# Attention without GpSimd's tensor work, the single query tile last, another cycle of steps, the first chunk's expert matmuls in the attention's plan

## The chip, the cores and the metric

The kernel runs on one core of a Trainium2 chip. The metric is the device time of one execution in microseconds (us), the median of several runs. A core has five engines, each of which takes its instructions in order: TensorE (PE in the profile; PEld is its weight load), VectorE (DVE), ScalarE (ACT), GpSimd (POOL) and SyncE (SP), which here only starts transfers. Engines wait for each other through semaphores. SBUF is the on-chip memory that all of them read and write; PSUM holds TensorE's results.

## The reference

```python
scores = scale * np.matmul(q, k.transpose(0, 1, 3, 2))       # (4, 8, 576, 576), head_dim 64
thresh = np.max(scores, axis=-1, keepdims=True) - tau
scores = np.where(scores >= thresh, scores, -1000000000.0)
scores = scores - np.max(scores, axis=-1, keepdims=True)
attn = np.exp(scores)
attn = attn / (np.sum(attn, axis=-1, keepdims=True) + 1e-09)
x = np.matmul(attn, v)                                        # then (2304, 512)
...
h = x @ w_in                                                  # expert 1: 512 -> 2048 -> 512
x = (np.maximum(h, 0.0) + alpha * np.minimum(h, 0.0)) @ w_out
h = x @ w_in2                                                 # expert 2
out = (h * (1.0 / (1.0 + np.exp(-h)))) @ w_out2
```

The weights of both experts arrive as 64-bit floats and are brought to 32 bits on the chip. Every 32-bit product of the experts is made of three matmuls of a rounded part and a rest (`TERMS`).

## The kernel before

**Attention.** The 32 heads are worked in 16 pairs. The 576 queries of a pair are nine tiles, t = 0 to 8: tiles 0 to 7 hold 128 queries of one head each, two by two (even t for the one head, odd t for the other), and tile 8, the single one, holds the last 64 queries of both. For each tile TensorE makes the scores (`qkmm`, L333) in PSUM; VectorE copies them to SBUF scaled and takes the row maximum in the same instruction (`maxi`, L347); ScalarE takes the exponential (`expo`, L360) and a threshold from maximum and tau (`thr`, L367); VectorE masks by the threshold and sums the row (`mask`, L373). TensorE then transposes the masked tile into PSUM (`trans`, L408) and ScalarE copies it to SBUF (`copy`, L123). The sums' reciprocals (`recip`, L382) are spread over 64 columns by a broadcast copy (`spread`, L388, on GpSimd) and are transposed too (`transr`, L414). TensorE multiplies with the values (`pv`, L442, in five steps; `pv8`, L449, for the single tile), and VectorE multiplies by the transposed reciprocals into `X` (`evac`, L456; `evac8`, L463).

**The order.** All of this stands in a manual schedule. `CYCLE` lists TensorE's steps for one turn, each with an offset in pairs: Q is a score step, T a bank of transposes, Tr and Rr the leftover columns and the spread reciprocals, P a value step. `line` repeats it over the pairs, and TensorE issues in exactly this order. `plan()` walks the engines in time, with a duration and a priority for every operation, and so sets the order of the other four. Before the change a pair's tiles come in the order 8, 0, 1, ... 7. Score tiles share two PSUM buffers (`psS`), so a score step waits for the row maxima of the tiles two places earlier.

**Other work in the plan.** Four of the eight weight tiles that the first expert needs first are converted during the attention (`conv`, `wconv`, WN = 4, from score step 60 on, every 12 steps). One conversion is a 0.5 MB transfer and nine operations: ScalarE L157, VectorE L159, L161, L163, ScalarE L165, L167, GpSimd L169 and L171, VectorE L173. The first token chunk of 512 is split into its two parts there too (`xh`, `xl`, L545 and L548).

**Experts.** The second part is left to the tile framework's scheduler, which orders all engines by its own estimates and may place its instructions among the attention's. A job is one of 2 experts, 4 groups of hidden units and 5 chunks of tokens (four of 512, one of 256). In a job each of the four hidden blocks takes 12 matmuls (`mm_h`, L202) into a PSUM tile of `psH` (4 buffers), an activation (`act1`: ScalarE L211, VectorE L212; `act2`: L221, L222), a split (L123, L119), and, three blocks later (`LAG`), the output matmuls (`ymm`, L590 or L599). Chunks are split by ScalarE and GpSimd (`xsplit`), and the remaining weights are converted here with the same `wconv`.

Of the kernel before, what the change touches and what calls it, by code (L numbers as in the profile page):

```python
# [8 lines left out]
F32 = mybir.dt.float32  # L9
# [14 lines left out]
G = 4  # L24
# [16 lines left out]
WT = 30  # L41
# [54 lines left out]
def attn_moe_moe(  # L96
# [52 lines left out]
    def wconv(stage, pool, wi, wo, g, j):  # L149
# [82 lines left out]
    wA, xs0 = [], {}  # L232

    with ExitStack() as pa:
# [9 lines left out]
        psS = ent(name="psS", bufs=2, space=PSUM)  # L244
# [24 lines left out]
        seq = [(i, t) for i in range(NP) for t in (8, 0, 1, 2, 3, 4, 5, 6, 7)]  # L269
# [114 lines left out]
        def spread(i, ch):  # L384
# [6 lines left out]
        line = [(x, i + o) for i in range(-1, NP + 1) for x, o in cycle if 0 <= i + o < NP]  # L391
# [80 lines left out]
        def conv(j, after):  # L472
            it = wconv(stage, (wpa, wpo)[j // NC], w1i, w1o, 0, j)
# [13 lines left out]
        op(("tauv",), "DVE", 0.3, -1, [("ld", 0, 1)], setv)  # L487
# [186 lines left out]
```

## Time and profile before

| | us |
|---|---|
| median of 3 runs (1094.64 to 1097.5) | 1095.68 |
| the profiled execution's own time | 1095.02 |
| span of its instructions in the profile | 1093.2 |
| TensorE busy | 1077.0 (99%) |
| VectorE, ScalarE, GpSimd busy | 745.0, 599.1, 413.6 |

The attention takes the first 307 us of the span and the experts the rest. "Busy" is the union of an engine's instructions; matmuls are pipelined and overlap in the record, so the pace of TensorE is read from start to start and not from the length of one. In a timeline a bracket behind a row names the time that the engine stood idle ahead of it, and what ended that.

### The profile page before, as it was taken

Reading aid. Unit: us, or ns where it says so; the run is one execution under the profiler, and the core shown is the slowest. Engines: PE = TensorE matmul, PEld = TensorE weight load, DVE = VectorE, ACT = ScalarE, POOL = GpSimd, SP = SyncE. Lnnn points to the kernel's source line nnn. Section 1 sums busy time; section 2 is a strip of 40 time slices with the busy share of each in tenths; the row PEclk is TensorE's granted clock in tenths of the full one; section 3 lists DMA queues with packets and bytes.
Section 4 is the critical chain, followed back from the end, with each engine's and each line's share of the span. In section 5 each row is a group of like instructions: output and inputs, shape, how many; then the busy total and the mean of one; then the engine's idle time right before and its main releaser. Section 6 shows DMA issues by size and latency. Waiting matters only on the chain.

```text
span 1093.2 us, 15460 instructions
## 1 busy us (share of the span) xinstructions
PE 1077.0 (99%) x5705; PEld 837.9 (77%) x5705; DVE 745.0 (68%) x1382; ACT 599.1 (55%) x1129; POOL 413.6 (38%) x339
## 2 busy tenths in 40 slices
PE   8999999999999999999999999999999999999998
PEld 5666656556767888888888888888888888888887
DVE  6989999989456677848755883764378568634343
ACT  5777878877555765535533553564555445334321
POOL 0100131320155566528525662662365346424210
PEclk8999999999999999999999999999999999999999
DMA  3212222211022222201110120121012002000112
GB/s 105 65 60 65 79 84 85 79 60 41 19 78 77 77 62 75 77 1 58 63 34 20 60 77 1 39 78 39 1 58 78 20 20 78 1 1 1 39 58 77
DMA packets 19259, 57.10 MB, mean 52 GB/s; under 512 B 2416, under 2 KB 2544, under 8 KB 19184
## 3 DMA queue, kind: packets, MB, share of 16 engines
q1 hardware_dynamic: 18880, 55.84, 15.8%
q8 instruction: 45, 0.74, 0.3%
q10 hardware_dynamic: 304, 0.28, 0.1%
q14 instruction: 30, 0.25, 0.1%
HBM read 51.39 MB, written 4.72 MB: 51 GB/s over the span
## 4 chain that ended last, share of the span: by engine, by line
PE 74%; DVE 6%; issue 3%; POOL 2%; ACT 2%; DMA 0%; DVEq 0%; POOLq 0%; ACTq 0%; SPq 0%
PE h L202 33%; PE y L599 18%; PE y L590 14%; PE s L333 3%; PE pv L442 3%; PE t L408 3%; DVE e L373 2%; POOL we L171 1%; DVE x L347 1%; DVE wa L161 1%; POOL wa L169 1%; DVE w L173 0%; ACT acc L228 0%; DVE wm L159 0%; DVE r L212 0%
## 5 line engine op out<-in xcount | busy, mean ns | idle before, releaser
L202 PE MATMUL h<-xs,w 128*128 128x512 f32 (+1 forms) x1920 | 431.1, 368 | 3.1 <-DVE r L212 3.1
L202 PEld LDWEIGHTS h<-xs,w 128*128 128x128 f32 x1920 | 337.8, 188 | 66.2 <-DVE r L212 4.9
L590 PE MATMUL y<-g,w 128*128 128x512 f32 (+1 forms) x960 | 215.0, 368 | 0.4 <-ACT acc L228 0.4
L599 PE MATMUL y<-w,g 128*128 128x512 f32 x864 | 213.7, 390 | 0.0
L590 PEld LDWEIGHTS y<-g,w 128*128 128x128 f32 x960 | 169.0, 188 | 31.6 <-ACT acc L228 0.7
L599 PEld LDWEIGHTS y<-w,g 128*128 128x128 f32 x864 | 160.7, 188 | 32.4
L119 DVE TENSOR_TENSOR g<-r,g 128x512 fp32r<-128x512 f32 (+1 forms) x160 | 140.7, 879 | 52.4 <-ACT g L123 51.1
L169 POOL TENSOR_TENSOR wa<-wa,w 128x512 f32<-128x512 f32 x64 | 84.0, 1313 | 207.3 <-ACT w L165 86.2
L119 POOL TENSOR_TENSOR xs<-acc,xs 128x512 fp32r<-128x512 f32 (+1 forms) x80 | 106.5, 1361 | 133.2 <-ACT xs L123 133.1
L123 ACT ACTIVATE g<-r 128x512 fp32r<-128x512 f32 (+1 forms) x160 | 94.0, 588 | 90.0 <-DVE r L222 46.6
L119 POOL TENSOR_TENSOR xs<-X,xs 128x512 fp32r<-128x512 f32 (+1 forms) x76 | 104.2, 1399 | 57.5 <-ACT xs L123 57.3
L347 DVE TENSOR_SCALAR_CACHE_REDUCE x<-s,nsc 128x576 f32<-128x576 f32 x144 | 112.4, 815 | 13.0 <-PE s L333 11.5
L360 ACT ACTIVATE e<-x,m 128x576 f32<-128x576 f32 x128 | 96.3, 781 | 43.5 <-DVE x L347 42.9
L373 DVE SCALAR_TENSOR_TENSOR e<-x,m,e 128x577 f32<-128x577 f32 x128 | 110.1, 881 | 8.1 <-ACT m L367 7.7
L222 DVE TENSOR_TENSOR r<-h,r 128x512 f32<-128x512 f32 (+1 forms) x80 | 50.7, 634 | 95.0 <-ACT r L221 94.9
L333 PE MATMUL s<-raw 64*128 64x288 f32 (+1 forms) x576 | 110.3, 437 | 5.1 <-DVE x L347 4.3
L388 POOL COPY rb<-m 128x256 f32<-128x256 f32 (+1 forms) x48 | 27.6, 576 | 211.8 <-PE t L414 100.3
L173 DVE TENSOR_TENSOR w<-we,wa 128x512 fp32r<-128x512 f32 x64 | 58.7, 918 | 61.1 <-POOL we L171 52.0
L221 ACT ACTIVATE r<-h 128x512 f32<-128x512 f32 (+1 forms) x80 | 43.8, 548 | 102.5 <-PE h L202 102.0
L171 POOL TENSOR_TENSOR we<-we,wm 128x512 f32<-128x512 f32 x64 | 93.6, 1462 | 13.7 <-ACT wm L167 13.1
L212 DVE SCALAR_TENSOR_TENSOR r<-r,neg,h 128x512 f32<-128x512 f32 (+1 forms) x80 | 55.0, 689 | 48.6 <-ACT r L211 48.4
L165 ACT ACTIVATE w<-wa 128x512 fp32r<-128x512 f32 x64 | 40.5, 633 | 82.2 <-DVE wa L161 75.4
(63 smaller groups left out, 1054.9 us busy)
## 6 DMA issues: line engine op xcount, KB each, us to landing
wraw<-in_w1i SPq DMA_DIRECT2D x16, 512.0 KB, 3.7
wraw<-in_w1o SPq DMA_DIRECT2D x16, 512.0 KB, 3.4
wraw<-in_w2i SPq DMA_DIRECT2D x16, 512.0 KB, 3.6
wraw<-in_w2o SPq DMA_DIRECT2D x16, 512.0 KB, 3.5
rv<-in_v SPq DMA_DIRECT2D x16, 480.0 KB, 3.4
raw<-in_q SPq DMA_DIRECT2D x15, 320.0 KB, 3.2
out<-o SPq DMA_DIRECT2D x18, 256.0 KB, 2.0
raw<-in_k SPq DMA_DIRECT2D x15, 288.0 KB, 2.8
```

Of the source, the lines that this page charges most:

```text
L119: le.tensor_tensor(out=lo, in0=src, in1=hi.bitcast(F32), op=ALU.subtract)
L123: e.activation(out=dst, in_=src, func=AF.Copy)
L169: nc.gpsimd.tensor_tensor(out=a, in0=a, in1=w[:, 0].bitcast(F32), op=ALU.subtract)
L171: nc.gpsimd.tensor_tensor(out=e, in0=e, in1=m, op=ALU.mult)
L173: V.tensor_tensor(out=w[:, 1], in0=e, in1=a, op=ALU.add)
L202: nc.tensor.matmul(ps[:, :n], w[c][:, a, fl * 128:(fl + 1) * 128], xs[c][:, b, :n], start=k == 0, stop=k == 3 * NC - 1,)
L333: T.matmul(SP[u + k][:, hf, :S // 2], RAW[i][p, 0, q], RAW[i][p, 1, c], start=True, stop=True)
L347: V.tensor_scalar(out=x.rearrange("p (a b) -> p a b", a=2), in0=SP[u][:, :, :S // 2], scalar1=nsc, scalar2=None, op0=ALU.mult, op1=ALU.min ...
L360: A.activation(out=ES[u], in_=xts[u % XB][:, 1:S + 1], func=AF.Exp, bias=mcol(u, 0), scale=-1.0)
L373: V.scalar_tensor_tensor(out=e, in0=x, scalar=mcol(u, 1), in1=e, op0=ALU.is_le, op1=ALU.mult, accum_out=mcol(u, 2))
L590: nc.tensor.matmul(ys[e][:, :n], w[NC + fl][:, a, e * 128:(e + 1) * 128], gt[:, c, :n], start=fl == 0 and k == 0, stop=fl == G - 1 and k == 2,
L599: nc.tensor.matmul(ys[s], gt[:, a, s * 128:(s + 1) * 128], w[NC + fl][:, c, :], start=fl == 0 and k == 0, stop=fl == G - 1 and k == 2,)
```

## The change

- The single tile comes last in a pair (order 0, 1, ... 8), and `CYCLE` is another list of the same steps. The first loads are ordered for it: the first 128 query columns come first, and tau's transfer is third instead of second on ScalarE's queue; pair 1's loads wait for the first score step.
- The broadcast of the reciprocals goes from GpSimd to ScalarE, as an activation.
- In the planned conversions GpSimd's two operations go to VectorE (the expert stage keeps them on GpSimd). The first four conversions start at score step 20, every 14 steps; the other four, of the output weights, are planned as well and start 4 score steps before the last.
- The first two chunks' splits are planned (ScalarE and VectorE).
- The first chunk's 48 hidden matmuls are operations of the plan (name "h"), which may fill TensorE's waits from the last row maxima on; their PSUM tiles come from `psS`, now two buffers of two blocks, which also takes the place of `psH` in all jobs.
- The expert stage's pools reuse memory with waits by tile (`reuse_waits="tile"`). A few planned durations and priorities differ.

```diff
-WI = 60
+WI = 20
+WT = 4
-WS = 12
+WS = 14
...
-    "P8:0 Q6:0 P1:-1 P2:-1 Rr1:-1 T1:0 Q8:1 T2:0 T3:0 "
+    "P0:-2 P1:-2 P2:-2 Q6:-1 T3:-1 T4:-1 T1:-1 Q8:-1 Tr8:-2 "
...
+        if e == "PE":
+            c = [n for n in c if n == seq[pe]] or [n for n in c if n[0] == "h"]
+            fill = [n for n in cand[e] if n[0] == "h"]
+            if fill and c != fill and ready[c[0]] > max(free[e], ready[fill[0]]) + ops[fill[0]][1]:
+                c = fill
...
-        nc.gpsimd.tensor_tensor(out=a, in0=a, in1=w[:, 0].bitcast(F32), op=ALU.subtract)
-        yield
-        nc.gpsimd.tensor_tensor(out=e, in0=e, in1=m, op=ALU.mult)
+        e2.tensor_tensor(out=a, in0=a, in1=w[:, 0].bitcast(F32), op=ALU.subtract)
+        yield
+        e2.tensor_tensor(out=e, in0=e, in1=m, op=ALU.mult)
...
-        seq = [(i, t) for i in range(NP) for t in (8, 0, 1, 2, 3, 4, 5, 6, 7)]
+        seq = [(i, t) for i in range(NP) for t in range(9)]
...
+            nc.sync.dma_start(raw(0)[:, 0, :128], src[0][:, :128])
+            nc.sync.dma_start(raw(0)[h0, 0, 128:], src[0][h0, 128:])
+            A.dma_start(raw(0)[h1, 0, 128:], src[0][h1, 128:])
             A.dma_start(sc[:, 0:1], tau[0:1].unsqueeze(0).to_broadcast([128, 1]))
...
-            P.tensor_copy(RS[i, ch][:, :n], stat(i)[:, 2, a:z].unsqueeze(2).to_broadcast([128, n, 64]))
+            A.activation(out=RS[i, ch][:, :n], in_=stat(i)[:, 2, a:z].unsqueeze(2).to_broadcast([128, n, 64]), func=AF.Copy)
...
-        for j in range(WN):
-            conv(j, [qk(WI + j * WS if j < NC else NU - WT)])
+        for j in range(NC + G):
+            conv(j, [qk(WI + j * WS if j < WN else NU - WT)])
...
+                need = [("h", f, c - 1)] if c else [("h", f - 1, NC - 1), ("max", NU - 2 + f // 2)]
+                op(("h", f, c), "PE", 0.68, 0, need + [("xl", 0, c), ("w", c, 9)], go, 0.9)
...
-        psH = ent(name="psH", bufs=4, space=PSUM)
...
-                ps = psH.tile([128, 512], F32, tag="h", name="h")
-                mm_h(ps, w, fl, xs, n)
+                if fl % 2 == 0:
+                    hp = hs0[fl] if (m, g, t0) == (1, 0, 0) else psS.tile([128, 2, 512], F32, tag="s", name="s")
+                ps = hp[:, fl % 2]
+                if (m, g, t0) != (1, 0, 0):
+                    mm_h(ps, w, fl, xs, n)
```

What stands on TensorE in the middle of the attention, for most of one cycle; `s` are scores, `t` transposes, `pv`, `p` and `q` value steps. Before:

```order
L333 MATMUL s<-raw 128x288 x4
L442 MATMUL pv<-pt,rv 64x512 x4
L414 MATMUL t<-ident,rb 128x128 x2
L408 MATMUL t<-ident,e 128x128 x4
L333 MATMUL s<-raw 128x288 x2
L408 MATMUL t<-ident,e 128x128 x12
L333 MATMUL s<-raw 128x288 x4
L442 MATMUL pv<-pt,rv 64x512 x2
L442 MATMUL pv<-px,rv 64x512 x2
L408 MATMUL t<-ident,e 128x128 x8
L333 MATMUL s<-raw 128x288 x4
L408 MATMUL t<-ident,z 128x128 x4
```

And after, on the same engine and in the same stage:

```order
L448 MATMUL pv<-pt,rv 64x512 x6
L339 MATMUL s<-raw 128x288 x4
L414 MATMUL t<-ident,e 128x128 x12
L339 MATMUL s<-raw 128x288 x2
L414 MATMUL t<-ident,z 128x128
L414 MATMUL t<-ident,e 128x128 x6
L420 MATMUL t<-ident,rb 128x128 x3
L339 MATMUL s<-raw 128x288 x4
L448 MATMUL pv<-pt,rv 64x512 x2
L455 MATMUL t<-p_1237,rv 64x64 x8
L455 MATMUL t<-q_1312,rv 64x64 x2
L448 MATMUL pv<-px,rv 64x512 x2
```

A whole cycle before has four runs of two-tile score steps, four of transposes (the single tile's scores, two matmuls, stand inside one of them) and three of value steps; after it has four, three and two.

The end of the attention on TensorE; `h` and, after, `s<-xs,w` are the first expert's hidden matmuls, `y` its output matmuls. Before:

```order
L408 MATMUL t<-ident,e 128x128 x4
L202 MATMUL h<-xs,w 128x512 x11
L408 MATMUL t<-ident,e 128x128 x2
L414 MATMUL t<-ident,rb 128x128 x2
L408 MATMUL t<-ident,e 128x128 x2
L202 MATMUL h<-xs,w 128x512 x5
L442 MATMUL pv<-pt,rv 64x512 x6
L414 MATMUL t<-ident,rb 128x128 x2
L442 MATMUL pv<-pt,rv 64x512 x2
L442 MATMUL pv<-px,rv 64x512 x2
L202 MATMUL h<-xs,w 128x512 x42
L590 MATMUL y<-g,w 128x512 x8
```

After:

```order
L448 MATMUL pv<-pt,rv 64x512 x6
L414 MATMUL t<-ident,z 128x128
L420 MATMUL t<-ident,rb 128x128
L448 MATMUL pv<-pt,rv 64x512 x2
L455 MATMUL t<-p_2973,rv 64x64 x8
L455 MATMUL t<-q_2994,rv 64x64 x2
L448 MATMUL pv<-px,rv 64x512 x2
L208 MATMUL s<-xs,w 128x512 x48
L616 MATMUL y<-g,w 128x512 x12
L208 MATMUL s<-xs,w 128x512 x12
L616 MATMUL y<-g,w 128x512 x24
L208 MATMUL s<-xs,w 128x512 x12
```

Before, 48 hidden matmuls stand among the last transposes and 42 follow the attention; after, no hidden matmul stands among the attention's steps, and 48 follow its last value step in one run.

A conversion in the middle of the attention. Before, on GpSimd, between the spread copies (`rb`):

```order
L388 COPY rb<-m 128x128
L388 COPY rb<-m 128x256
L169 TENSOR_TENSOR wa<-wa,w 128x512
L388 COPY rb<-m 128x256
L171 TENSOR_TENSOR we<-we,wm 128x512
L388 COPY rb<-m 128x128
```

After, on VectorE, where row maxima are L353, masks L379 and reciprocals L388:

```order
L379 SCALAR_TENSOR_TENSOR e,m<-x_119,m,e 128x577
L175 TENSOR_TENSOR wa<-wa,w 128x512
L353 TENSOR_SCALAR x_128,m<-s,nsc 128x576
L353 TENSOR_SCALAR x_119,m<-s,nsc 128x576
L379 SCALAR_TENSOR_TENSOR e,m<-x_122,m,e 128x577
L379 SCALAR_TENSOR_TENSOR e,m<-x_125,m,e 128x577
L379 SCALAR_TENSOR_TENSOR e,m<-x_128,m,e 128x577
L388 RECIPROCAL m<-m 128x4
L379 SCALAR_TENSOR_TENSOR e,m<-x_119,m,e 128x577
L353 TENSOR_SCALAR x_122,m<-s,nsc 128x576
L353 TENSOR_SCALAR x_125,m<-s,nsc 128x576
L177 TENSOR_TENSOR we<-we,wm 128x512
```

The two operations now stand between masks and maxima in VectorE's own queue, and GpSimd has nothing between its first instructions and the expert stage.

## Rows read from the trace of the kernel before

**Rows 1.** The page's busy time by engine (busy us, share of the span, instructions).

```profile
PE 1077.0 (99%) x5705; PEld 837.9 (77%) x5705; DVE 745.0 (68%) x1382; ACT 599.1 (55%) x1129; POOL 413.6 (38%) x339
```

**Rows 2.** Busy time of each engine in stretches of the attention: the stretch and its length in us, then busy us and (x instructions) of PE, PEld, DVE, ACT and POOL, the granted clock as a share of full speed, the DMA share and GB/s. The second and third are one cycle each, from one spread copy to the same copy of the next pair; the first covers six cycles, the last is the sixth of them.

```profile
121.46:233.47 112.01, 106.80 (x734) 63.79 (x732) 106.26 (x272) 89.87 (x176) 29.20 (x31) 0.98 0.23 75
87.42:104.44 17.02, 17.02 (x124) 10.57 (x123) 15.22 (x43) 13.30 (x27) 1.65 (x3) 1.00 0.20 63
121.46:138.48 17.02, 17.02 (x125) 10.55 (x123) 16.42 (x46) 14.41 (x29) 3.48 (x4) 1.00 0.21 68
210.38:233.47 23.09, 19.73 (x118) 10.46 (x117) 20.28 (x47) 16.27 (x33) 9.57 (x9) 0.93 0.12 36
```

**Rows 3.** The timeline of TensorE in one undisturbed cycle: start us, busy us, engine, line, tiles, count. The record counts each 32-bit score, value and small value matmul as two.

```profile
90.07 1.57 PE L333 MATMUL s<-raw 64*128 64x288 f32 x8
91.57 1.08 PE L442 MATMUL pv<-pt,rv 128*64 128x512 f32 x4
...
93.44 1.09 PE L408 MATMUL t<-ident,e 128*128 128x128 f32 x8
94.46 1.24 PE L333 MATMUL s<-raw 64*128 64x288 f32 x8
95.63 0.66 PE L408 MATMUL t<-ident,z 128*128 128x128 f32 x4
...
99.01 0.44 PE L408 MATMUL t<-ident,e 128*128 128x128 f32 x2
99.38 1.08 PE L442 MATMUL pv<-pt,rv 128*64 128x512 f32 x4
100.29 0.63 PE L449 MATMUL t<-p,rv 128*64 128x64 f32 x16
```

**Rows 4.** VectorE's maxima and masks between 20 and 260 us by line (count, then duration in ns, smallest, median and largest, and the first and last start), and four rows of the timeline of GpSimd and VectorE at one conversion.

```profile
L347 DVE TENSOR_SCALAR_CACHE_REDUCE x<-s,nsc x124: 782/816/821, 19.6 to 259.6; 128x576 f32<-128x576 f32 x124
L373 DVE SCALAR_TENSOR_TENSOR e<-x,m,e x108: 786/817/1824, 21.2 to 257.9; 128x577 f32<-128x577 f32 x108
```

```profile
138.48 0.83 POOL L388 COPY rb<-m 128x256 f32<-128x256 f32 x1 [0.70 <-PE t L414]
138.99 0.94 DVE L373 SCALAR_TENSOR_TENSOR e<-x,m,e 128x577 f32<-128x577 f32 x1
139.28 1.78 POOL L171 TENSOR_TENSOR we<-we,wm 128x512 f32<-128x512 f32 x1
139.86 1.82 DVE L373 SCALAR_TENSOR_TENSOR e<-x,m,e 128x577 f32<-128x577 f32 x1
```

**Rows 5.** VectorE's groups of the conversions between 20 and 260 us (line, engine, operation, tiles, shapes, count, busy us, mean ns of one, idle us before).

```profile
L161 DVE SCALAR_TENSOR_TENSOR wa<-wraw,wm 128x512 int32<-128x512 int32 x4 | 3.0, 738 | 0.0
L173 DVE TENSOR_TENSOR w<-we,wa 128x512 fp32r<-128x512 f32 x4 | 2.7, 680 | 0.0
L163 DVE TENSOR_SCALAR we<-wa 128x512 int32<-128x512 int32 x4 | 2.1, 520 | 0.0
L159 DVE TENSOR_SCALAR wm<-wm 128x512 int32<-128x512 int32 x4 | 1.7, 414 | 0.0
```

**Rows 6.** The timeline of GpSimd in the longest cycle.

```profile
217.40 5.88 POOL L119 TENSOR_TENSOR xs<-X,xs 128x512 fp32r<-128x512 f32 x4 [4.44 <-ACT xs L123]
```

**Rows 7.** The start: rows of the timeline (tau's transfer, its first user, the first mask, the second pair's second score step), and a stretch of TensorE alone (length, busy us and count of PE, clock, DMA share, GB/s).

```profile
1.34 0.87 ACTq L313 DMA_DIRECT2D sc<-in_tau  x1
5.63 0.15 DVE L137 TENSOR_SCALAR ge<-sc 128x1 f32<-128x1 f32 x1 [4.22 <-DMA sc<-in_tau]
7.96 0.82 DVE L373 SCALAR_TENSOR_TENSOR z<-x,m,z 128x577 f32<-128x577 f32 x1 [1.03 <-ACT m L367]
25.68 1.93 PE L333 MATMUL s<-raw 64*128 64x288 f32 x8
```

```profile
12.00:16.00 4.00, 4.00 (x16) 0.50 0.00 0
```

**Rows 8.** The end of the attention and the hand-over: rows of TensorE's timeline (the last pair's second score step; the first and the last of five groups that hold 48 hidden matmuls, of 18, 9, 5, 11 and 5; the last value step; the first rows of the experts), two stretches with the columns of rows 2, and the activation's two groups from 306 us on with the columns of rows 5.

```profile
274.58 1.24 PE L333 MATMUL s<-raw 64*128 64x288 f32 x8
...
285.19 4.38 PE L202 MATMUL h<-xs,w 128*128 128x512 f32 x18
...
300.39 1.39 PE L202 MATMUL h<-xs,w 128*128 128x512 f32 x5
...
305.71 1.03 PE L442 MATMUL pv<-px,rv 128*64 128x512 f32 x4
308.27 9.81 PE L202 MATMUL h<-xs,w 128*128 128x512 f32 x42 [1.53 <-DVE r L212]
317.92 1.98 PE L590 MATMUL y<-g,w 128*128 128x512 f32 x8
...
343.17 3.01 PE L202 MATMUL h<-xs,w 128*128 128x512 f32 x12 [1.32 <-DVE r L212]
```

```profile
306.00:345.00 39.00, 35.86 (x156) 28.39 (x153) 25.15 (x36) 22.43 (x41) 19.64 (x16) 1.00 0.26 83
345.00:1090.00 745.00, 743.67 (x3546) 625.75 (x3544) 460.60 (x639) 349.20 (x647) 342.11 (x253) 1.00 0.14 44
```

```profile
L212 DVE SCALAR_TENSOR_TENSOR r<-r,neg,h 128x512 f32<-128x512 f32 x64 | 47.3, 742 | 26.4 <-ACT r L211 26.2
L211 ACT ACTIVATE r<-h 128x512 f32<-128x512 f32 x64 | 37.5, 588 | 28.5 <-PE h L202 21.5 <-DVE g L119 5.2 <-PE pv L442 1.3
```

More of the change, by code (lines that the diff above doesn't have):

```diff
@@ L196, in xsplit, with mm_h @@
         return xs
-    def mm_h(ps, w, fl, xs, n):
-        k = 0
-        for c in range(NC):
+    def mm_h(ps, w, fl, xs, n, cs=range(NC)):
+        k = 3 * cs[0]
+        for c in cs:
             for a, b in TERMS:
@@ L230, in accum @@
             V.tensor_tensor(out=dst, in0=ps, in1=dst, op=ALU.add)
-    wA, xs0 = [], {}
+    psS = ctx.enter_context(tc.tile_pool(name="psS", bufs=2, space=PSUM))
+    wA, xs0, hs0 = [], [{}, {}], {}
     with ExitStack() as pa:
@@ L387, in spread @@
             RS[i, ch] = rbp.tile([128, 4, 64], F32, tag="rb", name="rb")
-            P.tensor_copy(RS[i, ch][:, :n], stat(i)[:, 2, a:z].unsqueeze(2).to_broadcast([128, n, 64]))
+            A.activation(out=RS[i, ch][:, :n], in_=stat(i)[:, 2, a:z].unsqueeze(2).to_broadcast([128, n, 64]), func=AF.Copy)
         cycle = [(x.split(":")[0], int(x.split(":")[1])) for x in CYCLE.split()]
-        line = [(x, i + o) for i in range(-1, NP + 1) for x, o in cycle if 0 <= i + o < NP]
+        line = [(x, i + o) for i in range(0, NP + 2) for x, o in cycle if 0 <= i + o < NP]
         banks = []
@@ L472, in conv @@
         def conv(j, after):
-            it = wconv(stage, (wpa, wpo)[j // NC], w1i, w1o, 0, j)
+            it = wconv(stage, (wpa, wpo)[j // NC], w1i, w1o, 0, j, V)
             prev = after
@@ L537, in attn_moe_moe @@
                 order["pv", i, kt] = ("pv", i, kt - 1)
-            op(("evac", i), "DVE", 0.62, 0, [("pv", i, KT - 1)], lambda i=i: evac(i), 0.78)
-        WOPS = [("SP", 0.6)] + [("ACT", 0.52), ("DVE", 0.34), ("DVE", 0.61), ("DVE", 0.34), ("ACT", 0.52), ("ACT", 0.52), ("POOL", 1.23), ("POOL", 1.23), ("DVE", 0.61)]
-        for j in range(WN):
-            conv(j, [qk(WI + j * WS if j < NC else NU - WT)])
-        for c in range(NC):
-            def hi0(c=c):
-                xs0[c] = bx.tile([128, 2, 512], F32R, tag="xs", name="xs")
-                one(A, xs0[c][:, 0], X[:, c, :512])
-            op(("xh", c), "ACT", 0.52, 9, [("evac", c), qk(NU - XO)], hi0)
-            op(("xl", c), "DVE", 0.61, 9, [("xh", c)], lambda c=c: V.tensor_tensor(out=xs0[c][:, 1], in0=X[:, c, :512], in1=xs0[c][:, 0].bitcast(F32), op=ALU.subtract))
+            op(("evac", i), "DVE", 0.62, -1, [("pv", i, KT - 1)], lambda i=i: evac(i), 0.78)
@@ new lines, in attn_moe_moe, with hi, lo @@
+        WOPS = [("SP", 0.6)] + [("ACT", 0.52), ("DVE", 0.34), ("DVE", 0.61), ("DVE", 0.34), ("ACT", 0.52), ("ACT", 0.52), ("DVE", 0.61), ("DVE", 0.61), ("DVE", 0.61)]
+        for j in range(NC + G):
+            conv(j, [qk(WI + j * WS if j < WN else NU - WT)])
+        for ch in range(2):
+            for c in range(NC):
+                t0, n = CH[ch]
+                def hi(ch=ch, c=c, t0=t0):
+                    xs0[ch][c] = bx.tile([128, 2, 512], F32R, tag="xs", name="xs")
+                    one(A, xs0[ch][c][:, 0], X[:, c, t0:t0 + 512])
+                def lo(ch=ch, c=c, t0=t0):
+                    x = xs0[ch][c]
+                    V.tensor_tensor(out=x[:, 1], in0=X[:, c, t0:t0 + 512], in1=x[:, 0].bitcast(F32), op=ALU.subtract)
+                src = [("evac", c), qk(NU - XO)] + ([("evac8", c), ("evac", HP + c), qk(NU - 1), ("xh", 0, c)] if ch else [])
+                op(("xh", ch, c), "ACT", 0.52, 9, src, hi, 0.72)
+                op(("xl", ch, c), "DVE", 0.61, 9, [("xh", ch, c)], lo, 0.8)
@@ new lines, in attn_moe_moe, with go @@
+        for f in range(G):
+            for c in range(NC):
+                def go(f=f, c=c):
+                    if f % 2 == 0 and c == 0:
+                        hs0[f] = psS.tile([128, 2, 512], F32, tag="s", name="s")
+                    mm_h(hs0[f - f % 2][:, f % 2], wA, f, [xs0[0][x] for x in range(NC)], 512, (c,))
+                need = [("h", f, c - 1)] if c else [("h", f - 1, NC - 1), ("max", NU - 2 + f // 2)]
+                op(("h", f, c), "PE", 0.68, 0, need + [("xl", 0, c), ("w", c, 9)], go, 0.9)
+                order["h", f, c] = need[0]
@@ L616, in attn_moe_moe @@
             oi = order.index((m, g))
-            if xs0:
-                xs = [xs0.pop(c) for c in range(NC)]
+            if (m, g) == (1, 0) and t0 < 1024:
+                xs = [xs0[t0 // 512][c] for c in range(NC)]
             else:
```

41 lines of the change are left out of this document (19 added, 22 removed), and 4 rows, old and new, of the table CYCLE.

## The prediction

> **What bounds the kernel now.** I read the page's busy times first, then the engines stretch by stretch, then TensorE's timeline inside one cycle of the attention, and last the two ends of the attention. TensorE is busy for 99% of the span [rows 1], so the question is what each of its microseconds is spent on. In the expert stage there is nothing to win: from 345 to 1090 us it stands idle for 1.3 us in all, at full clock [rows 8], and the change leaves it the same matmuls. In an undisturbed cycle of the attention it is busy for all of 17.02 us, while VectorE has 15.22 and ScalarE 13.30 [rows 2]. So TensorE's own stream sets the cycle. Six cycles in the middle take 112.01 us where six undisturbed ones would take 102.1: 9.9 us are lost there, and in the longest TensorE is idle for 3.4 us and its clock is at 0.93 [rows 2]. The sum below is made against the profiled execution's 1095.0 us, which is 0.7 under the median of the runs; I add 0.7 at the end.
>
> **The change part by part.**
>
> Fewer runs on TensorE. The pace is read from start to start. Eight transposes take 94.46 - 93.44 = 1.02 us and two take 99.38 - 99.01 = 0.37, so each costs 0.108 and the run itself about 0.15 [rows 3]. Eight value matmuls take 93.44 - 91.57 = 1.87 and four that are followed by more value work take 0.91 [rows 3], which leaves about the same 0.1 to 0.2 for a run of these. The new cycle has one run of transposes and one of value steps less and the same matmuls: -0.30 per cycle. Between the second score step of the second pair and that of the last lie 14 cycles: **-4.2**, from -2.8 to -5.6 with 0.1 to 0.2 for a run. One wait is left in the cycle: the score step behind the single tile takes 91.57 - 90.07 = 1.50 us where another takes 95.63 - 94.46 = 1.17 [rows 3]. After the change that step still stands behind the single tile and transposes (10, where there were 12), so I keep the 0.33.
>
> Conversions and chunk split off GpSimd. The 9.9 us of the six cycles go: a mask beside GpSimd's conversion took 1.82 us where the median is 0.82 [rows 4], and four chunk splits held GpSimd for 5.88 us [rows 6] with spread copies queued behind them: **-9.9**.
>
> Conversions on VectorE. A conversion now has six VectorE operations, the four of [rows 5] and two more like L173: 0.74 + 0.52 + 0.41 + 3 x 0.68 = 3.7, or 3.3 by starts, since each overlaps the next by some 0.07 to 0.08 (a maximum repeats at 0.74 and is recorded as 0.82 [rows 4]). VectorE is free for 16.7 - 15.1 = 1.6 us in a cycle of 16.7, and a conversion comes every 14 of 9 score tiles, every 1.56 cycles: 2.5 us of room for 3.3. It is short by 0.8, and I take 1.0 each, four times: **+4.0**. The lower end is 0: a cycle with VectorE at 16.42 was not a bit longer [rows 2]. The upper is all of it, 4 x 3.3 = +13.
>
> [...] The spread copies' effect is in the rows: the mask beside a copy of 0.83 us took 0.94, 0.13 more than the median [rows 4], so taking GpSimd's 1.65 us of copies per cycle away frees VectorE by about 0.1. [...]
>
> First chunk's split, four operations like L173 at 0.68 on VectorE inside two cycles with 3.2 us of room: **+0.5** (0 to 2.7). The second chunk's split comes after the last maxima, when VectorE has no more scores to take. The spread as an activation: three per cycle; even at GpSimd's 1.65 us they fit ScalarE's room of 17.02 - 13.30 = 3.7 [rows 2]: hidden, **0**, up to +2 if exponentials wait behind them.
>
> The start. Tau's transfer, which lets the first maximum go, started at 1.34 us and was waited for until 5.63 [rows 7]; third in its queue, it comes about half a microsecond later, so the first maximum starts near 6.7. By the new order VectorE has 11 maxima and 8 masks ahead of the second pair's second score step: 19 x 0.74 = 14.1, with reciprocals 14.3. The first mask of before waited 1.03 for ScalarE [rows 7]; I take four such waits: 25.0 where it was 25.68, **-0.7**. Pair 1's loads now wait for the first score step; from there they have some 17 us until that pair's own first one, and tau's transfer took 4.3 from start to landing: hidden. Without waits beyond 1.7 it is 22.7 (-3); with the clock at 0.50, as from 12 to 16 us of before [rows 7], the score steps take twice as long and it is 26.7 (+1).
>
> The end. From the last pair's second score step (274.58) to the last value step's end (305.71 + 1.03) are 32.2 us, of which 48 hidden matmuls take 48 x 0.23 = 11.0 (42 take 317.92 - 308.27 = 9.65): 21.1 for the attention [rows 8]. The new order works a pair later in the cycle. After that score step there is the rest of a cycle without the next pair's score step, 16.7 - 1.2 = 15.5, and a last turn of 26 transposes (3.1 with their runs), 12 value matmuls (2.8 at the rate of [rows 3]) and 8 with the 20 small ones (1.87 + 0.63 [rows 3]), 8.4, plus 1.0 of waits, since the order shows no hidden matmul that fills them: 24.9. **+3.8** (2.8 to 6).
>
> The hand-over. TensorE waited 1.53 and 1.32 us there, with 0.3 between [rows 8]. Now 48 hidden matmuls, 11 us, stand between the last value step and the first output matmul, and the activations run beside them; but VectorE has three conversions of the output weights in its queue, and behind them the activations. I leave 1.0 of 3.1: **-2.1** (-3 to +5).
>
> Sum: -4.2 - 9.9 + 4.0 + 0.5 + 0 - 0.7 + 3.8 - 2.1 = -8.6, which gives 1086.4 for the profiled execution and **1087** for the median.
>
> **The rivals.**
>
> All meshes. VectorE takes the conversions in its gaps (4.0 less), the 0.33 of each cycle goes (4.6 less) and the start is at its early end (2.3 less): **1076**. For it speaks the cycle with 16.42 us on VectorE that was not lengthened [rows 2]; against it that 15.1 + 3.3 / 1.56 = 17.2 us of VectorE do not go into 16.7.
>
> VectorE becomes the bound. It is at 90% now and at 103% by that last number while conversions run. Then the shorter stream of TensorE buys nothing (4.2 more) and a conversion costs 2.0 instead of 1.0 (4.0 more): **1095**, and up to 1100 with all of it on the path. That is mostly no change that a measurement of this kernel can tell, which begins at about 0.3%.
>
> Slower: the paired PSUM tiles. Before, a hidden block's PSUM tile was freed alone, four in turn; now two blocks share one, two in turn, and the first block of a new pair waits until VectorE has read the second of the pair before last. If that is on the path once in each of 39 jobs, the price is the activation, 0.59 + 0.74 = 1.3 us [rows 8], 52 us in all: **1139**. From 8.6 / 39 = 0.22 us per job it eats the gain. Against it: in the new order 12 or more output matmuls, 2.8 us, stand between a pair and its reuse.
>
> [...]
>
> **How the numbers follow.** The forecast of 1087 (1083 to 1092) has 0.60; all meshes 0.15; VectorE the bound 0.18; the paired tiles 0.05; the clock 0.02. Faster by over 0.3% means under 1092.4: 0.58 of the forecast, 0.15 and 0.03 of the third, 0.76. Slower, over 1099: 0.05 of the third and the last two, 0.12. The same: 0.12. The range leaves out the two slow cases, the top of the third and the lower half of the second: 1076 to 1096.
>
> **What would show it.** Right: undisturbed cycles of 16.6 to 16.9 us with TensorE busy throughout; cycles with a conversion of at most 17.7; masks never over 0.85 us in the attention; the second pair's second score step near 25; the attention's last value step ending near 289 without hidden matmuls before it; idle time of TensorE under 3 us from there to 345. Wrong: TensorE waiting for maxima in every cycle (VectorE the bound), hidden matmuls waiting for the activation in each job, or a clock below 1.00 after 345.

## The result and the profile after

The changed kernel takes 1104.42 us (median of four runs, 1103.04 to 1105.28) where the kernel before takes 1095.16 beside it: a ratio of 1.0083, 95% interval 1.0058 to 1.0108. It is slower by 0.8%; 1087 was forecast, with a range from 1076 to 1096.

The page's busy times of the changed kernel, against [rows 1]: TensorE has lost 2% of its share of the span, and GpSimd's tensor work starts behind the attention.

```profile
span 1103.5 us, 15284 instructions
...
PE 1072.2 (97%) x5705; PEld 835.7 (76%) x5705; DVE 750.3 (68%) x1402; ACT 606.8 (55%) x1177; POOL 353.8 (32%) x271
```

Cut where the prediction cut it: the 14 cycles from the second pair's second score step to the last pair's, the end up to the last value step, the 48 hidden matmuls, the hand-over, the expert stage. Windows of the changed kernel: length, then busy us of TensorE, its weight loads, VectorE, ScalarE, GpSimd, the granted clock, DMA share and GB/s.

```profile
25.05:255.80 230.75, 230.75 (x1708) 144.49 (x1709) 221.50 (x619) 201.77 (x426) 0.00 (x0) 1.00 0.23 73
255.80:280.18 24.38, 24.09 (x182) 14.30 (x180) 20.86 (x57) 20.69 (x43) 0.00 (x0) 1.00 0.18 64
280.18:291.20 11.02, 11.02 (x50) 9.12 (x49) 8.06 (x13) 5.62 (x10) 3.01 (x3) 1.00 0.55 180
291.20:345.00 53.80, 48.06 (x201) 38.36 (x200) 40.14 (x56) 31.47 (x57) 29.12 (x20) 0.97 0.20 63
345.00:1090.00 745.00, 728.82 (x3452) 609.72 (x3451) 439.54 (x599) 333.81 (x617) 320.73 (x243) 1.00 0.12 39
```

The attention did better than forecast and the expert stage far worse. The first row is 14 cycles of 16.48 us with TensorE busy in all of it; before they took 274.58 - 25.68 = 248.90 [rows 7, 8]. In the last row TensorE stands idle for 16.2 us, where [rows 8] has 1.3. Against the spans (1103.5 and 1093.2):

| part | before | after | difference | forecast |
|---|---|---|---|---|
| to the second pair's second score step | 25.68 | 25.05 | -0.6 | -0.7 |
| 14 cycles | 248.90 | 230.75 | -18.2 | -9.6 |
| the end, with 48 hidden matmuls | 32.16 | 35.40 | +3.2 | +3.8 |
| from there to the end of the span | 786.5 | 812.3 | +25.8 | -2.1 |

The last line begins at 306.74 before and at 291.20 after; from either on the same matmuls are left, all but 48 hidden ones. So 25.8 us were lost on the same work. TensorE's waits in the changed kernel, from 290 to 345 us and then from 345 to 1090 (total, times, longest). L208 is the hidden matmul, L616 and L625 are the output matmuls, L218 and L228 VectorE's step that reads a hidden block from PSUM in the first and second expert layer.

```profile
PE y L616 <- DVE g L125: 2.8, 2, 1.9
PE s L208 <- DVE r L218: 2.7, 1, 2.7
PE y L616 <- ACT g L129: 0.2, 1, 0.2
```

```profile
PE s L208 <- DVE r L218: 6.0, 4, 1.8
PE s L208 <- DVE r L228: 4.7, 4, 1.6
PE y L616 <- DVE acc L236: 2.7, 2, 1.3
PE y L625 <- DVE acc L236: 1.3, 1, 1.3
PE y L616 <- ACT acc L234: 1.0, 1, 1.0
PE y L625 <- DVE X L236: 0.5, 1, 0.5
```

Nine waits, 13.4 us, are hidden matmuls that wait for the reading of an earlier hidden block: the paired PSUM tiles, which the prediction gave 0.05. All waits together are 21.9 us; before, the same stretch has 3.5, of which 3.1 are in [rows 8]. One of them from the timeline of all engines (start, length, engine, line, operation, in brackets the idle time before and who ended it):

```profile
519.27 1.98 PE L208 MATMUL s<-xs,w 128*128 128x512 f32 x8
...
521.08 2.88 PE L616 MATMUL y<-g,w 128*128 128x512 f32 x12
...
522.61 0.69 ACT L163 ACTIVATE wm<-wraw 128x512 f32<-128x512 f32 x1 [2.44 <-POOL we L177]
...
523.19 1.08 ACT L217 ACTIVATE r<-s 128x512 f32<-128x512 f32 x2
...
523.79 0.69 DVE L167 SCALAR_TENSOR_TENSOR wa<-wraw,wm 128x512 int32<-128x512 int32 x1
...
524.52 0.43 DVE L169 TENSOR_SCALAR we<-wa 128x512 int32<-128x512 int32 x1
524.86 0.74 DVE L218 SCALAR_TENSOR_TENSOR r<-r,neg,s 128x512 f32<-128x512 f32 x1
...
525.66 1.19 PE L208 MATMUL s<-xs,w 128*128 128x512 f32 x4 [1.69 <-DVE r L218]
```

The block that the next pair waits for (the second of s_4961 in the listing below) ends one matmul, 0.23 us, before the output matmuls start: at 520.85. Its reading does not begin then. ScalarE is held until 522.61 by the first step of a weight conversion (L163), which waits for GpSimd, and the activation stands behind it; VectorE then has two more steps of the conversion (L167, L169) ahead of its own. Its step starts at 524.86 and ends at 525.60, 4.75 us after the block. TensorE had one hidden and 12 output matmuls to do meanwhile, until 525.66 - 1.69 = 523.97, which is 3.1 us. At 525.66 it goes on. The other eight waits look the same: in each an L163 that GpSimd had held stands just ahead of the activation on ScalarE, a conversion's step stands just ahead of VectorE's, and the reading ends 2.9 to 6.9 us after the block.

In program order on TensorE (the numbers tell the tiles apart) these blocks stand so:

```
1374 L208 MATMUL s_4961<-xs_4945,w_4000 128x512 [waits DVE_49]
...
1410 L208 MATMUL s_5022<-xs_4945,w_4000 128x512 [waits DVE_49]
...
1415 L208 MATMUL s_4961<-xs_4945,w_4000 128x512 [waits DVE_49]
...
1427 L208 MATMUL s_5103<-xs_5087,w_4000 128x512 [waits DVE_49]
```

Tile s_4961 gets its first block, then s_5022 its first but for one matmul, and only then s_4961 its second. In the code the second block of a pair comes behind the activation of the first, and its matmuls carry a wait for VectorE's reading of that first block. So two tiles stand filled at about the same time, both still to be read, when the next pair (s_5103) needs one.

### The profile page after: what moved, and what is told of

Same layout as the page of the kernel before. It is cut to its first block, busy times and chain, and to the rows that moved or that the text cites. A ratio compares the mean times of both kernels' runs of the same rounds, so it can differ in the third digit from the quotient of the medians.

```text
span 1103.5 us, 15284 instructions
## 1 busy us (share of the span) xinstructions
PE 1072.2 (97%) x5705; PEld 835.7 (76%) x5705; DVE 750.3 (68%) x1402; ACT 606.8 (55%) x1177; POOL 353.8 (32%) x271
## 4 chain that ended last, share of the span: by engine, by line
PE 73%; DVE 12%; POOL 6%; issue 5%; ACT 3%; DMA 0%; DVEq 0%; POOLq 0%; ACTq 0%; SPq 0%
PE s L208 25%; PE y L625 13%; PE y L616 11%; PE s L339 8%; PE t L414 7%; PE pv L448 6%; POOL we L177 3%; DVE g L125 2%; DVE wa L167 2%; DVE w L179 2%; POOL wa L175 2%; POOL xs L125 2%; DVE wm L165 1%; DVE r L218 1%; ACT w L171 1%
## 5 line engine op out<-in xcount | busy, mean ns | idle before, releaser
L208 PE MATMUL s<-xs,w 128*128 128x512 f32 (+1 forms) x1920 | 420.6, 371 | 13.3 <-DVE r L218 8.6
L208 PEld LDWEIGHTS s<-xs,w 128*128 128x128 f32 x1920 | 339.5, 190 | 81.0 <-DVE r L218 10.8
L175 POOL TENSOR_TENSOR wa<-wa,w 128x512 f32<-128x512 f32 x56 | 75.4, 1346 | 459.1 <-ACT w L171 346.2
L616 PE MATMUL y<-g,w 128*128 128x512 f32 (+1 forms) x960 | 210.1, 369 | 6.8 <-DVE g L125 2.8
L625 PE MATMUL y<-w,g 128*128 128x512 f32 x864 | 207.5, 390 | 1.8 <-DVE acc L236 1.3
L616 PEld LDWEIGHTS y<-g,w 128*128 128x128 f32 x960 | 167.3, 189 | 38.0 <-DVE g L125 3.7
L625 PEld LDWEIGHTS y<-w,g 128*128 128x128 f32 x864 | 160.9, 188 | 35.7 <-ACT r L227 1.5
L125 DVE TENSOR_TENSOR g<-r,g 128x512 fp32r<-128x512 f32 (+1 forms) x160 | 154.2, 978 | 27.1 <-ACT g L129 25.0
L228 DVE TENSOR_TENSOR r<-s,r 128x512 f32<-128x512 f32 (+1 forms) x80 | 49.0, 632 | 110.0 <-ACT r L227 109.8
L353 DVE TENSOR_SCALAR_CACHE_REDUCE x<-s,nsc 128x576 f32<-128x576 f32 x144 | 112.5, 816 | 12.9 <-PE s L339 11.9
L218 DVE SCALAR_TENSOR_TENSOR r<-r,neg,s 128x512 f32<-128x512 f32 (+1 forms) x80 | 53.8, 688 | 71.5 <-ACT r L217 71.3
L379 DVE SCALAR_TENSOR_TENSOR e<-x,m,e 128x577 f32<-128x577 f32 x128 | 99.7, 812 | 1.0 <-ACT m L373 1.0
L171 ACT ACTIVATE w<-wa 128x512 fp32r<-128x512 f32 x64 | 40.6, 635 | 97.2 <-DVE wa L167 74.4
L339 PEld LDWEIGHTS s<-raw 64*128 64x128 f32 (+1 forms) x576 | 59.6, 192 | 44.6 <-DVE e L379 12.2
L163 ACT ACTIVATE wm<-wraw 128x512 f32<-128x512 f32 x64 | 43.3, 677 | 87.5 <-POOL we L177 80.8
L227 ACT ACTIVATE r<-s 128x512 f32<-128x512 f32 (+1 forms) x80 | 41.3, 548 | 88.1 <-PE s L208 87.7
```

Of the source, the lines that this page charges most:

```text
L125: le.tensor_tensor(out=lo, in0=src, in1=hi.bitcast(F32), op=ALU.subtract)
L175: e2.tensor_tensor(out=a, in0=a, in1=w[:, 0].bitcast(F32), op=ALU.subtract)
L208: nc.tensor.matmul(ps[:, :n], w[c][:, a, fl * 128:(fl + 1) * 128], xs[c][:, b, :n], start=k == 0, stop=k == 3 * NC - 1,)
L339: T.matmul(SP[u + k][:, hf, :S // 2], RAW[i][p, 0, q], RAW[i][p, 1, c], start=True, stop=True)
L353: V.tensor_scalar(out=x.rearrange("p (a b) -> p a b", a=2), in0=SP[u][:, :, :S // 2], scalar1=nsc, scalar2=None, op0=ALU.mult, op1=ALU.min ...
L379: V.scalar_tensor_tensor(out=e, in0=x, scalar=mcol(u, 1), in1=e, op0=ALU.is_le, op1=ALU.mult, accum_out=mcol(u, 2))
```

## The experiments

Times are medians of four runs; ratios are to the kernel before, run beside them. It took 1095.09 beside the tile for each block, the pairs in the kernel before, the run without tile-wise waits and the output weights after the attention; 1095.28 beside the output weights along the attention, the two runs back on GpSimd and the kernel before with nothing of this on GpSimd; 1095.36 beside the other four. These differ by under 0.03%, so medians are compared across them.

**A tile for each hidden block.** The attention's tiles of two blocks are given up after the first job, and four tiles of one block take their place.

```diff
...
-                if fl % 2 == 0:
-                    hp = hs0[fl] if (m, g, t0) == (1, 0, 0) else psS.tile([128, 2, 512], F32, tag="s", name="s")
-                ps = hp[:, fl % 2]
...
+                    if psH is None:
+                        sS.close()
+                        psH = ent(name="psH", bufs=4, space=PSUM, side="right")
+                    ps = psH.tile([128, 512], F32, tag="h", name="h")
...
```

> The changed kernel, in which hidden blocks after the first job have a PSUM tile each again, four in turn; all else as changed. Theory (paired tiles): the hidden blocks' nine waits for the activation's two steps on VectorE, 13.3 us by the list of waits, go, and part of the output matmuls' waits behind them: 1084 to 1090. Rival (the conversions' steps on ScalarE and VectorE stand in front of the activations whatever the tiles): the waits move to other instructions and 1100 or more stays. Attention's last value step near 280 in both.

Measured: 1083.08, ratio 0.9892 (0.9875 to 0.9909), 21.3 us less than the changed kernel. TensorE's only waits from 290 to 1090 us, and its expert stage by the windows:

```profile
PE y L617 <- DVE g L125: 5.2, 2, 4.6
```

```profile
291.30:345.00 53.70, 48.49 (x203) 39.26 (x202) 43.17 (x58) 33.79 (x63) 31.28 (x22) 0.94 0.21 69
345.00:1070.00 725.00, 725.00 (x3461) 610.91 (x3460) 435.35 (x601) 332.01 (x613) 325.04 (x241) 1.00 0.12 39
```

From 345 us on TensorE is never idle. The activations are still late in that stage (one block's two steps start at 520.37 on ScalarE and only at 524.40 on VectorE), so the conversions in front of them cost nothing by themselves. The rest of this kernel's loss is at the hand-over.

**Pairs in the kernel before.** One edit the other way round:

```diff
-        psH = ent(name="psH", bufs=4, space=PSUM)
+        psH = ent(name="psH", bufs=2, space=PSUM)
...
-                ps = psH.tile([128, 512], F32, tag="h", name="h")
+                if fl % 2 == 0:
+                    hp = psH.tile([128, 2, 512], F32, tag="h", name="h")
+                ps = hp[:, fl % 2]
```

> The kernel before with one edit: hidden blocks in pairs, two PSUM tiles of two banks in turn. Theory (paired tiles): 13 to 20 us slower than the kernel before, 1107 to 1115, with waits of 1 to 2 us of hidden matmuls for VectorE's activation step in most of the jobs. Rival (the loss comes from how attention's new end joins the expert stage): within 3 us of the kernel before.

Measured: 1120.18, ratio 1.0226 (1.0203 to 1.0248): 25.1 us slower, more than the 13 to 20 expected. The first waits from 345 to 1090 us are nearly those of the changed kernel:

```profile
PE h L202 <- DVE r L212: 6.7, 5, 1.8
PE h L202 <- DVE r L222: 4.6, 4, 1.6
PE y L590 <- DVE acc L230: 2.7, 2, 1.4
```

The pairs alone cost it, without anything else of the change.

**Pairs with both blocks together.** The pair stays; only the order in the program is another, both blocks' matmuls and then both activations.

```diff
                 if fl % 2 == 0:
                     hp = hs0[fl] if (m, g, t0) == (1, 0, 0) else psS.tile([128, 2, 512], F32, tag="s", name="s")
+                    for x in range(2):
+                        if (m, g, t0) != (1, 0, 0):
+                            mm_h(hp[:, x], w, fl + x, xs, n)
                 ps = hp[:, fl % 2]
-                if (m, g, t0) != (1, 0, 0):
-                    mm_h(ps, w, fl, xs, n)
```

> The changed kernel, pairs kept, but the matmuls of both blocks of a pair stand in the program ahead of the activations of both. Theory (with one block's activation ahead of the second block, the second waits until the first has been read, since both lie in one tile): the waits for the activation nearly go, 1083 to 1092. Rival (two tiles in turn are too few, whatever the order): 1098 to 1106, with the same list of waits.

Measured: 1079.32, ratio 0.9851 (0.9837 to 0.9866), better than expected and the shortest median of this study: 25.1 us less than the changed kernel, the same amount that pairs cost the kernel before. TensorE's waits from 275 to 1090 us:

```profile
PE y L616 <- ACT acc L234: 2.2, 2, 1.5
PE y L616 <- DVE g L125: 0.6, 1, 0.6
```

So two tiles in turn are enough in this order. What cost the time was that the second block of a pair was kept apart from the first by the first one's activation. The reading is not earlier here: from 300 us on, VectorE's step ends a median of 6.6 us after a pair's last block, where the changed kernel has 2.4. What grew is TensorE's work between that block and the next use of its tile: at least 9.8 us, where the changed kernel has as little as 2.0 and the kernel before, with its four tiles, at least 10.0. From the first output matmul (290.01) to the end of the span (1076.5) are 786.5 us, as from 306.74 on in the kernel before.

**Without tile-wise waits** where the expert stage's buffers reuse the attention's room:

```diff
-        ent = lambda **k: pb.enter_context(tc.tile_pool(reuse_waits="tile", **k))
+        ent = lambda **k: pb.enter_context(tc.tile_pool(**k))
```

> The changed kernel without tile-wise waits where the expert stage's buffers reuse the attention's room; pairs stay. Theory (paired tiles): the expert stage from 345 us on is unchanged, 1100 to 1108. Rival (tile-wise waits let transfers and conversions start early and so put the queues in another order): 1085 or less.

Measured: 1103.65, ratio 1.0078 (1.0061 to 1.0096), as the changed kernel. This part of the change does nothing that can be measured.

**Output weights converted after the attention**, with a tile for each block:

```diff
-        for j in range(NC + G):
+        for j in range(WN):
             conv(j, [qk(WI + j * WS if j < WN else NU - WT)])
```

> As the run with a tile for each hidden block, and besides only the four input-weight conversions are planned with the attention; the first four output-weight conversions follow it, with GpSimd's two steps each, as in the kernel before. Theory (the planned conversions stand ahead of the first activations in VectorE's queue and cause the hand-over's waits of 6.4 us): 2 to 4 us less than the run with a tile for each hidden block. Rival (GpSimd is slower at them than VectorE, 2.7 us against 1.4 each): 3 to 10 us more.

Measured: 1083.01, ratio 0.9887 (0.9870 to 0.9905): no difference, and neither theory. The wait of 4.6 us for VectorE's split is gone, and another of 4.2 stands there, for a conversion (`w L171`). One queue was exchanged for another.

**Output weights converted along the attention**, with a tile for each block:

```diff
-            conv(j, [qk(WI + j * WS if j < WN else NU - WT)])
+            conv(j, [qk(WI + j * WS)])
```

> As the run with a tile for each hidden block, but the four output-weight conversions start along the attention like the input weights' (every 14 score tiles, the last at tile 118) and not at its end. Theory (at the hand-over VectorE works through conversions that stand ahead of the first activations): the 5.2 us that output matmuls wait there go, 1077 to 1080. Rival (VectorE is full in the attention: 15.9 us of 16.5 in the cycles of that run): each of the four lengthens its cycle by 1 to 3.3 us, 1083 to 1092, with TensorE waiting for maxima.

Measured: 1081.08, ratio 0.9868 (0.9854 to 0.9883). The time lies between the two ranges, and both theories hold in part. The 5.2 us of waits at the hand-over become 2.7, for ScalarE, whose first activation now stands behind a conversion that waits for its load:

```profile
287.54 0.66 ACT L163 ACTIVATE wm<-wraw 128x512 f32<-128x512 f32 x1 [7.10 <-DMA wraw<-in_w1i]
288.11 0.58 ACT L217 ACTIVATE r<-s 128x512 f32<-128x512 f32 x1
```

And the attention grew: from the first pair's evacuation to the last's are 282.8 - 43.1 = 239.7 us, against 280.6 - 42.7 = 237.9 with a tile for each block. Four more conversions in the attention cost 1.8 us, 0.45 each.

**Conversions back on GpSimd**, the two steps of the four input weights, with a tile for each block:

```diff
-            it = wconv(stage, (wpa, wpo)[j // NC], w1i, w1o, 0, j, V)
+            it = wconv(stage, (wpa, wpo)[j // NC], w1i, w1o, 0, j, nc.gpsimd if j < WN else V)
...
```

> As the run with a tile for each hidden block, but the two steps of each input-weight conversion that the change took from GpSimd are back on it. Theory (masks of 1.8 us beside GpSimd's conversion steps made the long cycles of the kernel before): 4 to 10 us slower, 1087 to 1093, with masks of 1.8 us. Rival (the long cycles came from the old order of steps): within 2 us, 1081 to 1085.

Measured: 1086.07, ratio 0.9914 (0.9897 to 0.9931), 3.0 us more than without, between the two ranges. The masks of this kernel and of the one with a tile for each block (least, median and greatest duration in ns, first and last start):

```profile
L380 DVE SCALAR_TENSOR_TENSOR e<-x,m,e x128: 783/814/1845, 8.5 to 271.9; 128x577 f32<-128x577 f32 x128
```

```profile
L380 DVE SCALAR_TENSOR_TENSOR e<-x,m,e x128: 787/816/822, 8.5 to 269.2; 128x577 f32<-128x577 f32 x128
```

The long masks come with GpSimd's conversion steps (up to 1.85 us) and go with them (at most 0.82).

**Spread copies back on GpSimd**, with a tile for each block:

```diff
-            A.activation(out=RS[i, ch][:, :n], in_=stat(i)[:, 2, a:z].unsqueeze(2).to_broadcast([128, n, 64]), func=AF.Copy)
+            P.tensor_copy(RS[i, ch][:, :n], stat(i)[:, 2, a:z].unsqueeze(2).to_broadcast([128, n, 64]))
...
```

> As the run with a tile for each hidden block, but the 48 spread copies are back on GpSimd. Theory (by the rows of the kernel before a copy costs a mask beside it 0.13 us, which TensorE's stream hides): 1082 to 1085. [...]

Measured: 1082.50, ratio 0.9884 (0.9869 to 0.9898): no difference. Between 40 and 250 us its 102 masks of `e` take 0.812 us in the mean, as in the changed kernel (0.812, 102 masks), which has nothing on GpSimd there; with the conversions on GpSimd it is 0.837 (101 masks), and the longest mask is 1.85 us where the median is 0.81.

**The kernel before with nothing of this on GpSimd, and with the conversions alone moved.** Two runs; the second leaves the spread copies where they were.

```diff
-        nc.gpsimd.tensor_tensor(out=a, in0=a, in1=w[:, 0].bitcast(F32), op=ALU.subtract)
+        e2.tensor_tensor(out=a, in0=a, in1=w[:, 0].bitcast(F32), op=ALU.subtract)
...
-            P.tensor_copy(RS[i, ch][:, :n], stat(i)[:, 2, a:z].unsqueeze(2).to_broadcast([128, n, 64]))
+            A.activation(out=RS[i, ch][:, :n], in_=stat(i)[:, 2, a:z].unsqueeze(2).to_broadcast([128, n, 64]), func=AF.Copy)
...
```

> The kernel before with two edits: the planned conversions on VectorE and the spread copies on ScalarE; its cycle, its single tile first and its expert stage stay. Theory (GpSimd's work made the long cycles): 7 to 10 us faster than the kernel before, 1085 to 1088; the new cycle of steps is then worth 5 us or so. Rival (VectorE with conversions is too full for the old order): 1093 to 1100, and the gain is the new cycle's.

> The kernel before with one edit: the planned conversions' two GpSimd steps on VectorE; spread copies stay on GpSimd. Theory (the run with both edits lost its time to the single tile's copies, which came late from ScalarE behind the spread copies; the conversions alone gain): 1 to 4 us faster than the kernel before, 1091 to 1094. Rival (the old cycle has no room on VectorE for the conversions): 1098 to 1108.

Measured: 1107.32, ratio 1.0103 (1.0088 to 1.0118), with both; 1089.73, ratio 0.9945 (0.9931 to 0.9960), with the conversions alone. Neither theory of the first run holds; the second run is a little better than its theory, and its rival falls. In the old order the conversions' move gives 5.6 us by itself, and the spread copies on ScalarE take 17.6 away again. TensorE's first wait from 25 to 320 us in the run with both, and one such place:

```profile
PE t L449 <- ACT q L123: 12.6, 8, 1.6
```

```profile
86.31 1.45 ACT L360 ACTIVATE e<-x,m 128x576 f32<-128x576 f32 x2
...
87.83 0.38 ACT L123 ACTIVATE q<-t 128x256 f32<-128x256 f32 x1
...
88.27 0.69 PE L449 MATMUL t<-p,rv 128*64 128x64 f32 x16 [1.57 <-ACT q L123]
```

The single tile's value step waits for a copy that ScalarE does behind two exponentials. The kernel before plans exponentials ahead of copies; the change turns that round and moves that step too. Which of the two makes the spread harmless was not tried apart.

**The new cycle alone**, with a tile for each hidden block and both kinds of work back on GpSimd (the last two edits to the changed kernel together):

> As the run with a tile for each hidden block, but the input-weight conversions' two steps and the spread copies are both on GpSimd as before; the new cycle of steps, the single tile last and the hidden blocks planned stay. Theory (the new cycle gives most, GpSimd's work 3 us): 1084 to 1088. Rival (the cycle needs GpSimd empty): 1092 or more.

Measured: 1084.76, ratio 0.9901 (0.9885 to 0.9918), as expected: 10.6 us of the 12.0 that the kernel with a tile for each block gains are there without ScalarE spreading and without VectorE converting the input weights. The chunk splits, which are off GpSimd in both, are part of the 10.6.

**Hidden matmuls early**, on top of the output weights along the attention:

```diff
...
+            if fill and pe > late and ready[fill[0]] <= free[e]:
+                return fill
```

Here `late` is the place of the last score step.

> As the run with output-weight conversions along the attention, but the planner places the first chunk's hidden matmuls as soon as they are ready after the last score step, ahead of the last pair's transposes and value steps. Theory (the last wait of 2.7 us at the hand-over comes from activations that start late): 1077 to 1079. Rival (VectorE's queue keeps the activations behind the last evacuation, which now ends 11 us later): 1081 to 1085, with the wait before the first output matmul.

Measured: 1079.66, ratio 0.9855 (0.9840 to 0.9869), 1.4 us less than without, between the theories. The output matmuls still wait 3.0 us in two pieces, as the rival had it, though for ScalarE and not for VectorE. What is gone is the low clock behind the one long wait: 0.50 from 303 to 305 us without this edit, 1.00 from 291 to 345 us with it.

## Why the prediction was wrong

**The step that failed** is the third rival, "the paired PSUM tiles", at 0.05, and the line "Against it: in the new order 12 or more output matmuls, 2.8 us, stand between a pair and its reuse." The mechanism was named rightly, and the output matmuls are there (521.08 to 523.97, 2.9 us). The price of the other side was wrong: I took the activation as 0.59 + 0.74 = 1.3 us, the durations of its two steps, as if it began when the block ends. It ends 4.75 us after the block, since its first step is queued behind a conversion's step that waits for GpSimd and its second behind two more. With 4.75 against 3.1, the cover fails by about the 1.7 us that TensorE waited. How late the buffer was read came from the queues, not from the duration of the instructions. That in the expert stage "there is nothing to win" hid that there was something to lose: four tiles in turn had covered the lateness.

I had also not seen why two tiles fill at once: the second block stands behind the first one's activation. That this order is the cause, and not the number of tiles, is shown by the run with both blocks together; the two blocks far apart on TensorE are read from the order. The rival's 52 us, one wait in each of 39 jobs, were too many: there are nine such waits, and the pairs cost 25.1 us.

Point by point, the rest:

- **Start**, -0.7: measured -0.6; the second pair's second score step at 25.05 where 25.0 was forecast. That was luck: the first maximum started at 7.42 and not near 6.7, VectorE waited for ScalarE 1.0 us in all and not four times 1.03, and it waited 3.6 us for TensorE's scores, which the sum had left out.
- **14 cycles**, -4.2, -9.9, +4.0 and +0.5: measured -18.2. The sizes that were off are the conversions and the chunk split on VectorE (4.5) and the wait of 0.33 that I kept in each of 14 cycles (4.6): without these the forecast is -18.7. That it then comes so near is in part luck. By [rows 3] eight value matmuls take 1.87 us and four take 0.91, which leaves 0.05 for a run of them and not 0.1 to 0.2. A cycle fell from 17.02 to 16.48; less the 0.33 that is 0.21 for the two runs, 2.9 in 14 cycles and not 4.2. The long cycles, 248.90 - 14 x 17.02 = 10.6 us, gave more than 9.9. Behind the single tile and its transposes a score step now takes 253.35 - 252.18 = 1.17 us, so the 0.33 is gone. TensorE was busy for all of 230.75 us, with VectorE at 221.50, 96%, so the four conversions cost nothing, though by my mean of 17.2 us in a cycle of 16.7 they did not fit. With eight of them the first costs appear, 0.45 each. This is the case "all meshes". The move by itself was -9.9 + 4.0 = -5.9, chunk split included; the conversions alone measured -5.6 in the old order and -3.0 in the new one.
- **Spread on ScalarE**, 0: right for the change as it stands, by the run that moves it back. But it hangs on the new order or the new priorities: in the old ones it costs 17.6 us, far above the bound of +2 that I gave.
- **The end**, +3.8: measured +3.2.
- **Hand-over**, -2.1 with +5 as its upper bound: waits of 5.7 us from 290 to 345 against 3.1, so about +2.6 and the low clock behind it. The cause named, conversions queued ahead of the activations, is what the runs show; it moves from queue to queue (VectorE 5.2, ScalarE 4.2 or 2.7), and it goes to 0.6 with both blocks together, where 2.2 of another kind are left: output matmuls that wait until ScalarE has read earlier output sums (`acc`, L234).
- **The clock** in the expert stage, 0.02: from 291 to 1090 us the changed kernel has it below 1.00 from 317 to 322 and from 444 to 448 only, two falls to 0.50 behind waits of 2.65 and 1.79 us; they follow from the waits and cost some 3.4 us.

Of the 25.8 us, 18.4 are more waits (21.9 against 3.5). Some 7 are not in the list of waits; about 3.4 of it is the low clock (below), and how the rest divides was not measured. In the run with both blocks together the whole 25.8 is gone.

## What to carry to other kernels

Here two halves of one buffer were one buffer to what set the waits, and the reader of the first half came between them: write both before the first is read. Before you cut the number of buffers that turn, read from the trace how long after the writer's end the reader really starts, behind everything else in its queue; cover that, not the reader's own duration. And work moved to an engine with room is free only if its place in that engine's order is right: the same spread copies cost nothing in one order and 17.6 us in another.

## What the hardware showed

After two of the changed kernel's waits TensorE's granted clock went from 1.00 to 0.50, but not at once: TensorE resumed at full clock (1.00 up to 317.75 and up to 444.00 us), and the clock fell afterwards (0.50 from 318.00 and from 444.25). Windows around the wait of 2.65 us that ended at 317.04, behind the one of 1.79 that ended at 443.58, and behind the one of 1.69 that ended at 525.66:

```profile
314.00:317.00 3.00, 0.39 (x2) 0.00 (x0) 1.88 (x4) 1.96 (x4) 1.01 (x1) 1.00 0.45 162
317.00:318.50 1.50, 1.46 (x5) 1.20 (x6) 1.50 (x3) 1.50 (x4) 0.00 (x0) 0.77 0.00 0
318.50:320.00 1.50, 1.50 (x5) 1.15 (x4) 0.78 (x2) 1.50 (x4) 0.19 (x1) 0.50 0.04 11
320.00:321.00 1.00, 1.00 (x4) 0.80 (x3) 0.22 (x1) 0.75 (x2) 1.00 (x1) 0.50 0.00 0
321.00:322.00 1.00, 1.00 (x6) 0.81 (x5) 0.64 (x1) 0.00 (x0) 1.00 (x2) 0.89 0.59 115
...
443.50:445.00 1.50, 1.42 (x4) 1.14 (x5) 0.80 (x3) 1.45 (x3) 1.02 (x1) 0.70 0.45 115
445.00:446.50 1.50, 1.50 (x5) 1.19 (x4) 1.50 (x4) 0.39 (x2) 0.00 (x0) 0.50 0.62 235
446.50:448.00 1.50, 1.50 (x5) 1.16 (x5) 1.50 (x4) 0.49 (x1) 0.00 (x0) 0.66 0.00 0
...
525.60:527.00 1.40, 1.34 (x6) 1.13 (x7) 1.40 (x3) 0.78 (x3) 1.40 (x2) 1.00 0.33 29
527.00:529.00 2.00, 2.00 (x11) 1.64 (x10) 2.00 (x4) 1.20 (x2) 0.82 (x1) 1.00 0.64 242
```

By the first rows such a fall costs 1.5 x 0.23 + 1.5 x 0.5 + 0.5 + 0.11 = 1.7 us on top of a wait of 2.65, and the second fall by its three rows as much; behind the wait of 1.69 there is none. In the kernel with a tile for each block the clock fell inside a wait, the one of 4.56 us that ended at 300.63:

```profile
295.60:300.50 4.90, 0.47 (x3) 0.05 (x1) 4.90 (x7) 0.70 (x2) 2.89 (x2) 0.81 0.01 2
300.50:302.00 1.50, 1.37 (x3) 1.16 (x4) 1.50 (x4) 0.79 (x2) 0.00 (x0) 0.50 0.00 0
```

So a wait can cost more than its own length, and the list of waits does not show it.
